# Letting Pool take the weights' low words, and letting the planner run Pool beside VectorE's largest-magnitude steps

## The chip, the cores and the metric

One core of one Trainium2 chip runs the whole kernel: causal attention followed by a feed-forward layer. The metric is device microseconds from the first to the last instruction of a launch. The median of three timed runs of the kernel before is 1076.19 us (1075.35 to 1078.62). The engines are named as in the profile: PE is TensorE, with PEld its weight loads, DVE is VectorE, ACT is ScalarE, POOL is GpSimd (the code calls it Pool), and SP is the engine that issues the transfers.

## The reference

```python
def _attn_ref(q, k, v, s):                      # q, k, v: 8 x 8 x 576 x 64, s: 8 x 8 x 576
    scores = (1.0 / np.sqrt(D)) * np.matmul(q, k.transpose(0, 1, 3, 2))
    cum = np.cumsum(np.maximum(s, 0.0), axis=-1)
    bias = -(cum[:, :, :, None] - cum[:, :, None, :])
    scores = np.where(causal, -1000000000.0, scores + np.minimum(bias, 0.0))
    attn = np.exp(scores - np.max(scores, axis=-1, keepdims=True))
    attn = attn / (np.sum(attn, axis=-1, keepdims=True) + 1e-09)
    return np.matmul(attn, v)

def _moe_ref(x, w_in, w_out):                   # x: 4608 x 512, w_in: 512 x 2048, w_out: 2048 x 512
    h = x @ w_in
    g = np.where(h > 0.0, h, np.exp(np.minimum(h, 0.0)) - 1.0)
    return g @ w_out
```

The attention's output, with its heads side by side, is the `x` of the second function. The two weight matrices arrive as 64-bit floats, everything else as 32-bit floats.

## The kernel before

**Stages.** The attention works on units of one batch, one pair of heads and one head of the pair. Softmax is done in blocks of 128 queries (`softmax_block`): PE makes the scores in a bank `sc` (line 969), DVE adds the mask and takes the row's extreme (line 972, written `CUSTOM_DVE_ANT_0` in the profile and `ISA` in lists of the order, with a second short instruction that reads the accumulator), ACT takes the exponential (line 977), and the block is scaled and cut into two half-precision parts by POOL, DVE or ACT (lines 1016 to 1030). There are 352 such blocks. SP turns the parts by a transfer, and PE multiplies them with the values into a bank `av` (line 1131). The feed-forward layer works on 12 chunks of 384 tokens; a chunk runs over 16 slices `f` of the hidden width. Chunk 0 is done in full precision (`hidden_native`, lines 1301 and 1346). The others are done with each operand cut into two half-precision parts: 12 matmuls of 384 columns for `h` (line 1317), then the activation through ACT and DVE (lines 1281 to 1335: `g`, `h`, `gg`), then 9 matmuls of 512 columns into `o` (line 1354).

**The weights.** 32 pieces of 128 x 512 weights (16 of `w_in`, 16 of `w_out`) are loaded as pairs of 32-bit words by `load_unit`. ACT turns the high word of each into a scaled float (line 638). DVE takes the low word to its top three bits (line 641: multiply by 2 to the -29, clip at 7). DVE joins the two (line 644). Then the piece's largest magnitude is taken by `peak`: on DVE as a `TENSOR_REDUCE` (line 575), or on ACT with an accumulator (line 578). `peak` also serves the values (`vs` and `va`), on DVE alone. When all 32 pieces are there, `weight_scales` makes common scales, and `split_unit` cuts every piece into two half-precision parts `wp` (ACT or POOL for the high part, DVE for the low part at line 659). Only then can chunk 1 and the later ones run.

**What sets the order.** Nothing is ordered by hand. Each step is given to `plan.op` as a list of ways, and a way is an engine, a cost in ns and the code. `Plan.issue` keeps a clock of its own for each engine. For each step it takes the way that would end first, and then it issues the step that could start first (a lower priority number goes first among equals); the order that comes out on each engine is the program's. Two rules of this planner matter here. The planner takes DVE's work with operands in SBUF (named `"DVE-SB"`) and Pool's work to exclude each other: a `port` clock holds the end of the last of either kind, and a step of either kind may start only a little ahead of it (240 ns for `"DVE-SB"`, 120 ns for `"Pool"`). Way `"DVE"` is the same engine without that rule. Costs on DVE count 1.3 times when ways are compared. A change of one cost or way therefore moves the order of all later work on every engine.

Engines work through their instructions in this order, so one that waits holds up all that stand behind it on its engine.

Of the kernel before, what the change touches and what calls it, by code (L numbers as in the profile page):

```python
# [15 lines left out]
ALU = mybir.AluOpType  # L16
# [65 lines left out]
class Plan:  # L82
# [40 lines left out]
    def op(self, prio, ways, reads=(), writes=(), late=()):  # L123

        o = Op()
        o.ways, o.prio, o.filler = ways, (prio, len(self.ops)), False
        o.after, o.before, o.behind, o.bufs, o.new = set(late), [], [], set(), []
        firsts = set()
        for accesses, write in ((reads, False), (writes, True)):
            for a in accesses:  # L130
                b, part = a if isinstance(a, tuple) else (a, None)
                if not b.parts and b not in o.bufs:

                    o.new.append((b, self.place(b)))
                    b.first = o
                firsts.add(b.first)
                if b not in o.bufs:
                    o.bufs.add(b)
                    b.users += 1
                for key, (writers, readers) in b.parts.items():  # L140
                    if part is None or key is None or key == part:
                        o.after.update(writers)
                        if write:
                            o.after.update(readers)
                writers, readers = b.parts.setdefault(part, ([], []))
                if write:
                    if part is None:
                        b.parts = {None: ([o], [])}
                    else:
                        b.parts[part] = ([o], [])  # L150
                else:
                    readers.append(o)
        o.after.discard(o)
        firsts -= o.after | {o}
        for d in o.after:
            d.before.append(o)
        for d in firsts:
            d.behind.append(o)
        o.left, o.ready = len(o.after) + len(firsts), {}
        self.ops.append(o)  # L160
        return o
# [139 lines left out]
def act_s(n):  # L301

    return 205 + n / 1.2
# [26 lines left out]
def kernel(  # L330
# [43 lines left out]
    op = plan.op  # L374
    act, dve, pool, pe_ = nc.scalar, nc.vector, nc.gpsimd, nc.tensor

    def load(prio, dst, src, reads, writes, nbytes, late=(), lag=LAG):
        return op(prio, [("SP", SP_COST, lambda: nc.sync.dma_start(dst(), src()), lag, nbytes)],
                  reads, writes, late)
# [167 lines left out]
    def weight(f, kind):  # L547
        return (w_all[f // W_GROUP], (f, kind)), lambda: w_all[f // W_GROUP].v[:, f % W_GROUP, kind]
# [23 lines left out]
    def peak(prio, n, src, reads, at, axis=mybir.AxisListType.X, aside=None, also=()):  # L572

        col = slice(at, at + 1)
        ways = [("DVE-SB", 100 + 1.04 * n, lambda: dve.tensor_reduce(
            peaks.v[:, col], src(), axis, ALU.max, apply_absolute_value=True))]
        if aside is not None:
            ways.append(("ACT", 480 + n / 1.2, lambda: act.activation(
                aside(), src(), AF.Abs, accum_out=peaks.v[:, col])))
        op(prio, ways, reads, [(peaks, at), *also])  # L580
# [45 lines left out]
    def load_unit(f, kind, src):  # L626

        prio = W0 + WD * f
        a, n = src.shape[1], f"{'io'[kind]}{f}"
        place, value = weight(f, kind)  # L630
        if wide:
            raw = plan.buf(sb, [P, 512, 2], U32, f"w_{n}", tag="io", bufs=N_IO)
            load(prio, lambda: raw.v.rearrange("p (a n) t -> p a (n t)", a=a),
                 lambda: src.bitcast(U32), [], [raw], P * 4096, urgent if f >= N_FREE else ())

            op(prio, [("ACT", act_s(512), lambda: act.activation(
                raw.v[:, :, 1].bitcast(F32), raw.v[:, :, 1].bitcast(F32),
                AF.Prelu, scale=2.0**-112, alpha=2.0**32))], [], [(raw, 1)])  # L640
            op(prio, [("DVE-SB", 430.0, lambda: dve.tensor_scalar(
                raw.v[:, :, 0], raw.v[:, :, 0], 2.0**-29, 7.0, ALU.mult, ALU.min))],
               [], [(raw, 0)])
            op(prio, [("DVE-SB", 700.0, lambda: dve.scalar_tensor_tensor(
                value().bitcast(U32), raw.v[:, :, 1], 3, raw.v[:, :, 0],
                ALU.logical_shift_left, ALU.bitwise_or))], [(raw, 0), (raw, 1)], [place])
        else:
            load(prio, lambda: value().rearrange("p (a n) -> p a n", a=a), lambda: src,
                 [], [place], P * 2048, urgent)
        peak(prio, 512, value, [place], (A_IN, A_OUT)[kind] + f,  # L650
             aside=(lambda: raw.v[:, :, 0].bitcast(F32)) if wide else None, also=[(raw, 0)] if wide else [])
# [11 lines left out]
    def load_weights(f0, f1):  # L663
        wi = w_in.rearrange("(c p) f -> p c f", p=P)
        wo = w_out.rearrange("(f p) (a m) -> f p a m", p=P, a=1)
        for f in range(f0, f1):
            fs = slice(f * P, (f + 1) * P)
            load_unit(f, 0, wi[:, :, fs])
            load_unit(f, 1, wo[f])
# [33 lines left out]
    def prepare_low(u):  # L703

        b, j, prio = u.b, u.j, u.prio
        u.vs = vs[u.turn]
        u.k, clear = (k_first, None) if (b, j) == (0, 0) else low_keys(u.tag)
        u.q = plan.buf(sb, [P, 2 * LOW], F32, f"ql_{u.tag}", tag="qs", bufs=2)
        heads, h0 = slice(2 * j, 2 * j + 2), b * H + 2 * j
        at = slice(HB, HB + 1)  # L710
        load(prio, lambda: u.k.v[:HB], lambda: kT[b, :HB, heads, :LOW], [], [(u.k, "k")], P * LOW * 4)
        load(prio, lambda: u.q.v[:HB], lambda: qT[b, j, :HB, : 2 * LOW], [], [(u.q, "q")], P * LOW * 4)
        op(prio if b or j else -10, [("Pool-M", pool_1(2 * LOW), lambda: pool.memset(u.q.v[HB:], 1.0))],
           [], [(u.q, "ones")])
        if (b, j) > (0, 0):
            op(prio, clear, [], [(u.k, "sums")])

            src = aux if (b, j) == (0, 1) else aux_dram
            o = load(prio, lambda: u.k.v[at],
                     lambda: src.v[h0 : h0 + 2, 0, :LOW],  # L720
                     [(src, 0)], [(u.k, "sums")], 2 * LOW * 4)
        if (b, j) == (0, 1):
            urgent.append(o)
        load(prio, lambda: u.vs.v, lambda: vb[b, j, :, :n_low], [], [u.vs], P * n_low * D * 4)
        peak(prio, n_low * D, lambda: u.vs.v, [u.vs], A_LOW + b * NP + j, mybir.AxisListType.XY)
# [98 lines left out]
    def group_values(u):  # L824

        at = groups.index((u.b, u.blocks[0] > 0))
        prio, first, col = u.prio - V_AHEAD, A_GROUP + at * (NP + 1), 4 + 2 * at
        home = w_parts[NG - 1] if at == 0 else w_all[(at - 1) % 2]
        va = plan.buf(sb, [P, NP, 2 * (NQ + 1), D], F32, f"va_{at}", tag=home.key[1])
        for j in range(NP):  # L830
            load(prio + j, lambda j=j: va.v[:, j], lambda j=j: vb[u.b, j, :, 1:], [], [(va, j)], P * 2 * (NQ + 1) * D * 4)
            peak(prio, 2 * (NQ + 1) * D, lambda j=j: va.v[:, j], [(va, j)], first + j, mybir.AxisListType.XY)
        scales_of(prio, [(first, NP + 1)], col)
        back = scales.v.bitcast(U32)
        op(prio, [("DVE-SB", 100.0, lambda: power(
            back[:, col + 1 : col + 2], back[:, col : col + 1], 2 * 127 - 15))], [(scales, col)], [(scales, col + 1)])
        return va, col
# [600 lines left out]
    while rows:  # L1438
        chunk, left = [], TMAX
        while left:  # L1440
            b, late, r, n = rows.pop(0)
            if n > left:
                rows.insert(0, (b, late, r + left, n - left))
                n = left
# [79 lines left out]
```

## Time and profile before

| what | value |
|---|---|
| timed runs of the kernel before | 1075.35, 1076.19, 1078.62 us |
| span of the profiled execution (the profile names no other time of that execution) | 1076.1 us |
| instructions in the profile | 19708 |
| HBM read and written | 79.66 and 19.32 MB, 92 GB/s over the span |
| transfers in the core's main queue | 155.27 MB, 58.5% of 16 DMA engines' span |
| chain that ended last | PE 70%, DVE 16%, issue 5%, DMA 4%, ACT 2%, POOL 2% |

The busy time of an engine counts the time in which at least one of its instructions runs. Matmuls overlap: one of 384 columns is listed with some 328 ns although the next one starts 162 ns after it. A busy PE can thus still have gaps of up to that length between starts. The chain of waits is followed back from the last instruction, and the waits of an engine name what ended its idle time.

### The profile page before, as it was taken

What the parts mean: (1) busy time and instruction counts of PE and PEld (TensorE: products, weight loads), DVE (VectorE), ACT (ScalarE), POOL (GpSimd) and SP (SyncE); (2) the same over time, 40 slices, a digit from 0 to 9 for tenths busy, and PEclk for the clock granted to TensorE, in tenths of its full rate; (3) what the DMA queues carried; (4) which work ended last, traced back from release to release, by engine and by line L of the source; (5) the groups of instructions that cost most, each with busy time, mean ns of one, the idle gap of its engine ahead of it and who ended that gap; (6) DMA issues with size and microseconds to landing.
All of it is one profiled execution on the core that took longest, in us unless ns stands there. A gap on an engine that the chain in (4) does not pass through costs nothing.

```text
span 1076.1 us, 19708 instructions
## 1 busy us (share of the span) xinstructions
PE 1028.8 (96%) x6014; PEld 597.0 (55%) x6014; DVE 859.3 (80%) x2216; ACT 640.2 (59%) x1511; POOL 443.2 (41%) x687
## 2 busy tenths in 40 slices
PE   8899999899799999999999999999999999999998
PEld 7555555345455555555555555555555655555554
DVE  7787988998788988898898888988898998442433
ACT  5787675547566666655656666665556566444443
POOL 6542443525365645454535545444444544000000
PEclk9999999899899999999999999999999999999999
DMA  6776889526667675675579675867765567210000
GB/s 192 216 223 203 213 213 203 139 65 142 172 149 193 149 171 136 169 179 147 120 168 191 144 162 137 195 159 167 170 168 143 143 156 148 52 60 1 30 1 30
DMA packets 295097, 156.52 MB, mean 145 GB/s; under 512 B 214200, under 2 KB 269776, under 8 KB 294992
## 3 DMA queue, kind: packets, MB, share of 16 engines
q1 hardware_dynamic: 294992, 155.27, 58.5%
q8 instruction: 48, 0.79, 0.3%
q14 instruction: 57, 0.47, 0.2%
HBM read 79.66 MB, written 19.32 MB: 92 GB/s over the span
## 4 chain that ended last, share of the span: by engine, by line
PE 70%; DVE 16%; issue 5%; DMA 4%; ACT 2%; POOL 2%; SPq 1%; DVEq 0%; POOLq 0%; ACTq 0%
PE o L1354 24%; PE h L1317 23%; PE sc L969 8%; PE av L1131 5%; DVE p L1030 4%; PE o L1346 3%; PE h L1301 2%; DVE xl L1270 2%; DVE h L1326 2%; DVE wp L659 1%; DVE gg L1335 1%; DVE p L972 1%; PE trl L791 1%; DMA T<-p 1%; DMA stq<-in_qT_dram 1%
## 5 line engine op out<-in xcount | busy, mean ns | idle before, releaser
L1317 PE MATMUL h<-xh,wp 128*128 128x384 f16 x1408 | 394.1, 329 | 19.4 <-DVE gg L1335 14.0
L1354 PE MATMUL o<-wp,gg 128*128 128x512 f16 x1584 | 390.6, 382 | 0.0
L1317 PEld LDWEIGHTS <-wp 128*128 128x128 f16 x2112 | 198.0, 98 | 177.0 <-issue 35.8
L1317 PE MATMUL h<-xl,wp 128*128 128x384 f16 x704 | 230.8, 328 | 3.9 <-DVE xl L1270 3.9
L1354 PEld LDWEIGHTS <-gg 128*128 128x128 f16 x1584 | 147.2, 99 | 154.0 <-issue 6.8
L1281 ACT ACTIVATE g<-h,cs 128x384 f32<-128x384 f32 x176 | 101.8, 578 | 156.3 <-PE h L1317 145.4
L977 ACT ACTIVATE p<-p,mn 128x192 f32<-128x192 f32 (+1 forms) x232 | 144.2, 622 | 56.6 <-DVE mn L972 49.2
L1326 DVE SCALAR_TENSOR_TENSOR h<-g,cs,h 128x384 f32<-128x384 f32 x176 | 108.5, 617 | 86.8 <-ACT g L1288 85.7
L1030 DVE SCALAR_TENSOR_TENSOR p<-p,sm,p 128x512 f16<-128x512 f32 (+3 forms) x237 | 168.9, 736 | 3.2 <-POOL p L1022 1.1
L1330 ACT ACTIVATE gg<-h 128x384 f16<-128x384 f32 x155 | 75.4, 487 | 93.2 <-DVE h L1326 91.6
L969 PE MATMUL sc<-kh,qs 128*128 128x192 f32 (+2 forms) x272 | 120.0, 444 | 7.7 <-DVE mn L972 7.3
L972 DVE CUSTOM_DVE_ANT_0 p<-sc,maskw 128x192 f32<-128x192 f32 (+1 forms) x232 | 109.6, 480 | 18.8 <-PE sc L969 14.3
L1022 POOL TENSOR_SCALAR p<-p,sm 128x512 f16<-128x512 f32 (+3 forms) x120 | 79.5, 670 | 95.5 <-DVE sm L983 34.0
L1335 DVE SCALAR_TENSOR_TENSOR gg<-h,gg 128x384 f16<-128x384 f32 x176 | 96.9, 550 | 22.0 <-ACT gg L1330 19.3
L969 PE MATMUL sc<-k,q 128*128 128x192 f32 (+2 forms) x272 | 84.4, 313 | 0.5 <-DMA q<-qs 0.5
L411 POOL TENSOR_TENSOR k<-stk,kh 64x576 fp32r<-64x576 f32 x49 | 73.1, 1492 | 24.4 <-ACT kh L392 19.9
L969 PEld LDWEIGHTS sc<-kh,qs 128*128 128x128 f32 x272 | 52.4, 192 | 35.6 <-DVE mn L972 14.5
L1288 ACT ACTIVATE g<-g 128x384 f32<-128x384 f32 x134 | 69.9, 522 | 3.7
L1026 ACT ACTIVATE p<-p,sm 128x512 f16<-128x512 f32 (+3 forms) x100 | 57.4, 594 | 18.5 <-DVE sm L983 8.2
L411 POOL TENSOR_TENSOR qs<-stq,qs 64x512 fp32r<-64x512 f32 (+1 forms) x46 | 52.4, 1139 | 34.0 <-ACT qs L392 23.5
L390 POOL TENSOR_SCALAR qs<-stq 128x256 fp32r<-128x256 f32 (+1 forms) x43 | 24.3, 566 | 88.8 <-PE sc L969 57.5
L1131 PE MATMUL av<-T,v 128*64 128x256 f16 (+5 forms) x896 | 60.2, 286 | 0.0
(179 smaller groups left out, 1414.1 us busy)
## 6 DMA issues: line engine op xcount, KB each, us to landing
stk<-in_kT_dram SPq DMA_DIRECT2D x64, 288.0 KB
va<-in_vb_dram SPq DMA_DIRECT2D x32, 320.0 KB
stq<-in_qT_dram SPq DMA_DIRECT2D x40, 256.0 KB
w_i<-in_w_in_dram SPq DMA_DIRECT2D x16, 512.0 KB
w_o<-in_w_out_dram SPq DMA_DIRECT2D x16, 512.0 KB
out_dram<-ost SPq DMA_DIRECT2D x32, 256.0 KB
x_dram<-x_None SPq DMA_DIRECT2D x20, 288.0 KB
q<-qs SPq DMA_DIRECT2D x40, 128.0 KB
```

Source lines behind the costliest of these rows:

```text
L411: ("Pool", pool_2(n), lambda: pool.tensor_tensor(dst(), src(), hi(), ALU.subtract)),
L969: pe_.matmul(view(sc.v[:, :cw]), l, r, start=n == 0, stop=n == len(pairs) - 1)
L972: op(prio, [("DVE", 84 + dve_p(cw), lambda i=i, sc=sc: dve.tensor_tensor_reduce(pt.v[:, i * cw : (i + 1) * cw], sc.v[:, :cw], mv(i * cw, c ...
L977: op(prio, [("ACT", 480 + w / 1.2, lambda: act.activation(pt.v[:, :w], pt.v[:, :w], AF.Exp, bias=mn.v[:, n - 1 : n], scale=-1.0, accum_out ...
L1022: ("Pool", 160 + 1.04 * n, lambda part=part: pool.tensor_scalar(part(t16, 0), own(part), sm.v[:, r], 1.0, ALU.mult, ALU.mult)),
L1030: ("DVE-SB", dve_2(n), lambda part=part: dve.scalar_tensor_tensor(part(t16, 1), own(part), sm.v[:, r], part(t16, 0), ALU.mult, ALU.subtract)),
L1131: pe_.matmul(av.v[w.h * HB : (w.h + 1) * HB, dst], w.values.v[:, w.h, kb, v], part(w, kb, m), start=kb == 0 and m == 0 and v == 0, stop=kb ...
L1281: op(side, [("ACT", act_c(TC) + (0 if native else 90), lambda: act.activation(g.v[:, :TC], hp.v[:, :TC], AF.Exp, scale=1.0 if native else ...
L1317: pe_.matmul(hp.v[:, :TC], weight_part(f, 0, part)[1]()[:, c * P : (c + 1) * P], xx.v[:, c, :TC], start=(c == 0 and m == 0), stop=(c == NC ...
L1326: op(side, [("DVE", dve_p(TC), lambda: dve.scalar_tensor_tensor(hp.v[:, :TC], g.v[:, :TC], by(2 if sign[0] else 1), hp.v[:, :TC], ALU.mult ...
L1335: op(side, [("DVE", dve_p(TC), lambda: dve.scalar_tensor_tensor(gg.v[:, 1, :TC], hp.v[:, :TC], 2.0**-DOWN, gg.v[:, 0, :TC], ALU.mult, ALU. ...
L1354: pe_.matmul(acc[i].v, gg.v[:, g, tb], weight_part(f, 1, part)[1](), start=(f == 0 and m == 0), stop=(f == NF - 1 and m == 2),)
```

## The change

There are two edits. In `peak` the DVE way is renamed from `"DVE-SB"` to `"DVE"`, with the same cost and the same instruction: the planner no longer keeps Pool's work apart from it. In `load_unit` the step on the low words gets a second way: Pool at 660 ns, with the same arithmetic on the same words.

```diff
@@ def peak
-        ways = [("DVE-SB", 100 + 1.04 * n, lambda: dve.tensor_reduce(
+        ways = [("DVE", 100 + 1.04 * n, lambda: dve.tensor_reduce(
             peaks.v[:, col], src(), axis, ALU.max, apply_absolute_value=True))]
@@ def load_unit
-            op(prio, [("DVE-SB", 430.0, lambda: dve.tensor_scalar(
-                raw.v[:, :, 0], raw.v[:, :, 0], 2.0**-29, 7.0, ALU.mult, ALU.min))],
-               [], [(raw, 0)])
+            op(prio, [
+                ("DVE-SB", 430.0, lambda: dve.tensor_scalar(
+                    raw.v[:, :, 0], raw.v[:, :, 0], 2.0**-29, 7.0, ALU.mult, ALU.min)),
+                ("Pool", 660.0, lambda: pool.tensor_scalar(
+                    raw.v[:, :, 0], raw.v[:, :, 0], 2.0**-29, 7.0, ALU.mult, ALU.min)),
+            ], [], [(raw, 0)])
```

All lines behind the second edit stand three lower than before (line 972 becomes 975); the low words' step is line 642 on DVE and line 644 on Pool.

The planner gives 22 of the 32 low words' steps to Pool and leaves 10 on DVE. The largest magnitudes of the weights, of which DVE had 16 and ACT 16, now stand 22 on DVE and 10 on ACT. The other ways change in small numbers: over the whole program DVE has 2218 instructions before and 2224 now, ACT 1209 and 1190, POOL 692 and 707, and PE 10334 and 10336 (two more of the matmuls that only fill time at the start).

The first place is on POOL, at the second weight piece (`w_o_289` is its buffer; `pl` and `p` are softmax blocks, `v` a part of the values). Before:

```order
L990 TENSOR_SCALAR pl_1_295<-pl_1_295,sml_1_303 128x128
L990 TENSOR_SCALAR p_174<-p_174,sml_1_303 128x320
L402 TENSOR_SCALAR v_0_0_0_397<-va_134,scales 128x5x64
L402 TENSOR_SCALAR v_1_0_0_407<-va_134,scales 128x5x64 x2
L538 MEMSET p_87 128x64
```

Now:

```order
L993 TENSOR_SCALAR pl_1_295<-pl_1_295,sml_1_303 128x128
L993 TENSOR_SCALAR p_174<-p_174,sml_1_303 128x320
L644 TENSOR_SCALAR w_o_289<-w_o_289 128x512
L402 TENSOR_SCALAR v_0_0_0_402<-va_134,scales 128x5x64
L402 TENSOR_SCALAR v_1_0_0_414<-va_134,scales 128x5x64 x2
L538 MEMSET p_87 128x64
```

The low words' step stands between the scaling of softmax blocks, which waits for DVE's reciprocals, and the values.

The second place is on DVE, where the weights are cut after the common scales are known (`wp` are the parts, `wa` the pieces; `h`, `g` and `gg` belong to chunk 1; line 972 is a softmax block). Before, from the tenth of the 32 cuts on:

```order
L1326 SCALAR_TENSOR_TENSOR h_2_2380<-g_2_2411,cs_2238,h_2_2380 128x384
L659 SCALAR_TENSOR_TENSOR wp_2271<-wa_1049,scales,wp_2271 128x512 x2
L1335 SCALAR_TENSOR_TENSOR gg_2_2444<-h_2_2380,gg_2_2444 128x384
L1326 SCALAR_TENSOR_TENSOR h_3_2423<-g_3_2446,cs_2238,h_3_2423 128x384
L659 SCALAR_TENSOR_TENSOR wp_2271<-wa_1049,scales,wp_2271 128x512 x2
L1335 SCALAR_TENSOR_TENSOR gg_3_2461<-h_3_2423,gg_3_2461 128x384
L972 ISA p_174,mn_2_1_0_3_2472<-sc_2_1_0_3_0_2245,maskw 128x288
L972 ISA mn_2_1_0_3_2472 128x1
L659 SCALAR_TENSOR_TENSOR wp_2271<-wa_1049,scales,wp_2271 128x512 x2
L659 SCALAR_TENSOR_TENSOR wp_2302<-wa_1428,scales,wp_2302 128x512 x2
```

Now, from the third cut on:

```order
L662 SCALAR_TENSOR_TENSOR wp_2171<-wa_430,scales,wp_2171 128x512 x4
L1295 TENSOR_SCALAR g_0_2306<-g_0_2306 128x384
L662 SCALAR_TENSOR_TENSOR wp_2208<-wa_1006,scales,wp_2208 128x512
L1329 SCALAR_TENSOR_TENSOR h_0_2275<-g_0_2306,cs_2183,h_0_2275 128x384
L662 SCALAR_TENSOR_TENSOR wp_2208<-wa_1006,scales,wp_2208 128x512 x2
L1338 SCALAR_TENSOR_TENSOR gg_0_2332<-h_0_2275,gg_0_2332 128x384
L1329 SCALAR_TENSOR_TENSOR h_1_2302<-g_1_2336,cs_2183,h_1_2302 128x384
L662 SCALAR_TENSOR_TENSOR wp_2208<-wa_1006,scales,wp_2208 128x512 x2
L1338 SCALAR_TENSOR_TENSOR gg_1_2356<-h_1_2302,gg_1_2356 128x384
L662 SCALAR_TENSOR_TENSOR wp_2208<-wa_1006,scales,wp_2208 128x512 x3
```

Before, the 32 cuts stand between the 89th and the 94th softmax block; now all 32 stand behind the 88th with no block between them.

The third place is on PE, at the attention's last products. The number at the end of `h` is the slice `f` of the tenth chunk (chunk 9). Before:

```order
L1131 MATMUL av_3_1_2_11846<-T_3_1_2_11793,v_3_0_2_11532 64x64
L1354 LDWEIGHTS gg_11_11822
L1354 MATMUL o_2_11178<-wp_2302,gg_11_11822 128x512
L1354 LDWEIGHTS gg_11_11822
L1354 MATMUL o_2_11178<-wp_2302,gg_11_11822 128x512
L1354 LDWEIGHTS gg_11_11822
L1354 MATMUL o_2_11178<-wp_2302,gg_11_11822 128x512
L1317 LDWEIGHTS wp_2343
L1317 MATMUL h_13_11884<-xh,wp_2343 128x384
```

Now:

```order
L1134 MATMUL av_3_1_2_11923<-T_3_1_2_11869,v_3_0_2_11611 64x64
L1320 LDWEIGHTS wp_2256
L1320 MATMUL h_15_11899<-xh,wp_2256 128x384
L1320 LDWEIGHTS wp_2256
L1320 MATMUL h_15_11899<-xl,wp_2256 128x384
L1320 LDWEIGHTS wp_2256
```

Behind the last product of the attention stood 420 matmuls into `h` and 327 into `o`; now 390 and 306 stand there. The chunk is some two and a half slices further on when the attention ends.

## The prediction, made before the changed kernel ran

> **What bounds the kernel now.** I read the page's first part, then the busy times by stage, then the waits of PE, then the end of the chain.
>
> ```profile
> span 1076.1 us, 19708 instructions
> ...
> PE 1028.8 (96%) x6014; PEld 597.0 (55%) x6014; DVE 859.3 (80%) x2216; ACT 640.2 (59%) x1511; POOL 443.2 (41%) x687
> ```
>
> ```profile
> core 0: us, PE busy (x) PEld busy (x) DVE busy (x) ACT busy (x) POOL busy (x), PEclk, DMA share, GB/s
> 0.00:90.00 90.00, 80.40 (x496) 55.26 (x497) 73.19 (x252) 63.46 (x203) 47.33 (x122) 1.00 0.71 211
> 90.00:180.00 90.00, 89.54 (x357) 49.85 (x356) 76.51 (x195) 58.97 (x147) 32.39 (x51) 1.00 0.80 209
> 180.00:240.00 60.00, 52.75 (x244) 26.60 (x243) 55.69 (x113) 32.37 (x65) 27.71 (x33) 0.94 0.46 115
> 240.00:720.00 480.00, 456.34 (x2779) 267.23 (x2778) 417.91 (x1115) 298.13 (x721) 237.66 (x341) 0.99 0.68 160
> 720.00:930.00 210.00, 207.96 (x1365) 123.27 (x1364) 183.91 (x453) 125.08 (x262) 93.82 (x135) 1.00 0.64 152
> 930.00:1076.00 146.00, 141.84 (x782) 74.77 (x779) 52.11 (x92) 62.21 (x116) 4.26 (x6) 1.00 0.07 23
> ```
>
> PE is full from 90 to 180 us (89.54 of 90) and again from 720 us on (207.96 of 210; after 930 almost nothing but feed-forward matmuls is left). It has room in the other three stages: 9.6 us up to 90, 7.2 from 180 to 240, 23.7 from 240 to 720, and gaps shorter than a matmul's listed length come on top (its record outlasts the start of the next). In those stages DVE is the next fullest, with 81%, 93% and 87%, while POOL is at 53% and 36% in the two stages that read weights.
>
> ```profile
> PE h L1317 <- DVE gg L1335: 14.0, 18, 3.1
> PE sc L969 <- DVE mn L972: 7.8, 10, 2.5
> PE h L1317 <- DVE xl L1270: 3.9, 6, 1.5
> ```
>
> These are PE's three longest waits (us in total, times, longest), all for DVE. So I read the kernel as PE's sum of matmuls plus gaps that DVE's order sets. A change can gain only what closes such gaps; PE's own work stays, since its list has the same matmuls.
>
> **What the change takes off DVE.** The step itself:
>
> ```profile
> L641 DVE TENSOR_SCALAR w_i<-w_i x16: 398/428/651, 19.7 to 167.3; 128x512 uint32<-128x512 uint32 x16
> L641 DVE TENSOR_SCALAR w_o<-w_o x16: 409/434/1640, 28.5 to 175.2; 128x512 uint32<-128x512 uint32 x16
> ```
>
> ```profile
> L575 DVE TENSOR_REDUCE peaks<-wa 128x1 f32<-128x512 f32 x16 | 10.8, 677 | 0.2
> ...
> L641 DVE TENSOR_SCALAR w_o<-w_o 128x512 uint32<-128x512 uint32 x16 | 9.4, 589 | 2.0 <-DMA w_o<-in_w_out_dram 2.0
> ...
> L641 DVE TENSOR_SCALAR w_i<-w_i 128x512 uint32<-128x512 uint32 x16 | 7.2, 450 | 1.1 <-DMA w_i<-in_w_in_dram 1.1
> ```
>
> The 32 steps cost 9.4 + 7.2 = 16.6 us, 0.519 each, against medians of 0.428 and 0.434: a few are stretched. 22 go to Pool, 22 x 0.519 = 11.4 us. The ten that stay I take at the median, 0.9 us less in all. Together 12.3 us leave DVE. Six more largest magnitudes come to it from ACT, 6 x 0.677 = 4.1 us. The planner fills the rest of the room: summing each engine's list at the means of the groups by line and shape, other work that moves to DVE up to the last softmax block is 19.8 us, and 8.5 us move away. The largest of it:
>
> ```profile
> L1024 DVE TENSOR_SCALAR p<-p,sm 128x512 f16<-128x512 f32 (+3 forms) x52 | 26.2, 506 | 1.5 <-DVE sm L983 0.3
> ...
> L1292 DVE TENSOR_SCALAR g<-g 128x384 f32<-128x384 f32 x58 | 26.1, 451 | 10.7 <-ACT g L1281 10.6
> ...
> L410 DVE TENSOR_TENSOR k<-stk,kh 64x576 fp32r<-64x576 f32 x15 | 11.6, 773 | 1.1 <-POOL kh L390 0.7 <-ACT kh L392 0.3
> ...
> L418 DVE COPY tl<-trl 128x128 f32<-128x128 f32 (+2 forms) x21 | 7.9, 377 | 6.3 <-PE trl L791 4.6 <-PE trl L775 1.4
> ...
> L1145 DVE TENSOR_SCALAR x_None<-av,scales 128x512 f32<-128x512 f32 x9 | 6.7, 747 | 5.0 <-PE av L1131 4.8
> ```
>
> Twelve more copies out of the banks (4.9 us by their shapes), six more rests of q and k (4.7), six more scalings of softmax blocks (3.2), four more outputs of the attention (2.5); nine fewer steps on `g` (4.1). Net on DVE up to the last block: -12.3 + 4.1 + 19.8 - 8.5 = +3.1 us. Up to the 100th block, where the weights have just been cut, the same sum is -12.3 + 4.1 - 0.6 = -8.8 (the -0.6 is the other work), and up to the 280th it wavers between -5 and 0, of which I take -1.5. So DVE is relieved early, and the planner gives it back later, with ACT and POOL as partners.
>
> **What this does to the end.** Two estimates, since the bound changes at 720 us.
>
> ```profile
> 0.00:180.00 180.00, 34.95 (x176) 1.00 0.76 210
> 180.00:720.00 540.00, 89.32 (x384) 0.98 0.66 155
> ```
>
> ```profile
> L972 DVE CUSTOM_DVE_ANT_0 p<-sc,maskw,mn x64: 500/513/519, 114.7 to 919.7; 128x288 f32<-128x288 f32 x64
> ```
>
> ```profile
> L1131 PE MATMUL av<-T,v x896: 192/273/404, 142.4 to 932.6; 128*64 128x256 f16 x44, 128*64 128x192 f16 x38, 128*64 128x64 f16 x26, 128*64 128x512 f16 x24
> ```
>
> ```profile
> 960.86 1.95 PE h L1317 x12
> 962.81 1.94 PE o L1354 x9
> ```
>
> The first fence is the softmax line alone by stages: (176 + 384) / 2 instructions a block make 280 blocks before 720 us; the last starts at 919.7, and the attention's last product at 932.6. The fourth gives PE's pace: 1.95 / 12 = 0.1625 us for a matmul into `h`, 1.94 / 9 = 0.2156 into `o`.
>
> - If DVE's list sets when the attention ends, the end of attention comes 3.1 us later. Behind the last product stand 30 fewer matmuls into `h` and 21 fewer into `o`: 30 x 0.1625 + 21 x 0.2156 = 4.9 + 4.5 = 9.4 us less. Sum 3.1 - 9.4 = -6.3.
> - If PE is the bound from the 280th block on, what counts is the state there: DVE 1.5 us ahead, and feed-forward matmuls worth 1.1 us more already issued (counted in PE's lists at the pace above). Sum -1.5 - 1.1 = -2.6.
>
> I take the middle, -4.4: against the execution's own span, 1076.1 - 4.4 = **1071.7 us**. The span is 0.1 us below the median of the timed runs (1076.19), so the same figure stands for the median. About 0.3%, 3.2 us, is what a measurement of this kernel can tell from no change; the forecast lies just beyond it.
>
> **The Pool step's price.** No uint32 work on POOL is in the trace, nor a step of two words. The nearest rows:
>
> ```profile
> L390 POOL TENSOR_SCALAR qs<-stq 128x512 fp32r<-128x512 f32 x21 | 14.2, 675 | 46.9 <-DMA stq<-in_qT_dram 19.2 <-PE sc L969 17.6 <-issue 6.3
> ...
> L411 POOL TENSOR_TENSOR qs<-stq,qs 64x512 fp32r<-64x512 f32 x28 | 37.2, 1329 | 32.5 <-ACT qs L392 23.5 <-DVE sm L982 4.7 <-PE sc L969 1.5
> ...
> L402 POOL TENSOR_SCALAR wp<-wa,scales 128x512 f16<-128x512 f32 x17 | 15.5, 932 | 2.4 <-DVE scales L614 2.4
> ```
>
> I take 0.675, the row of the same operation and size; 1.329, the two-operand row, is the far end, and 0.45, what DVE needs, the near one. At 0.675 the 22 steps are 14.9 us in 180 us in which POOL works 79.7, beside other work. The joining of the words (line 644 before) now waits for Pool. DVE keeps its order, so behind a waiting join stand softmax steps (line 972), for which ACT's exponentials and PE's next scores wait. Per step, 1.329 - 0.675 = 0.65 us would be exposed at most, 22 x 0.65 = 14.4 us; at 0.45 nothing more is won, since the planner counts 0.66 anyway.
>
> [...]
>
> **The renamed way.** It costs and wins nothing by itself if Pool's work really runs beside it:
>
> ```profile
> 44.47 1.47 POOL L990 TENSOR_SCALAR pl<-pl,sml 128x320 f32<-128x320 f32 x1
> ...
> 45.87 0.67 DVE L575 TENSOR_REDUCE peaks<-wa 128x1 f32<-128x512 f32 x1
> ```
>
> The reduction began within Pool's step and took 0.67 us, its mean (677 ns). So the planner's new freedom is real, and its worth is inside the lists above.
>
> **The rivals.**
>
> *No change (1076).* The relief ends at the 100th block; from 90 to 180 us PE is full, and from 720 us on again. If the gaps between (7.2 + 23.7 us) depend on chains rather than on DVE's sum, the early 8.8 us become slack and the tail's 9.4 us come back as a later end of attention. For it speaks that DVE's whole list is not shorter (2224 against 2218 instructions); against it that PE's longest waits are for DVE. It gives 1076.1 - 0.
>
> *Slower (1082).* Pool's steps hold up DVE.
>
> ```profile
> 133.88 1.40 POOL L411 TENSOR_TENSOR k<-stk,kh 64x576 fp32r<-64x576 f32 x1 [1.55 <-ACT kh L392]
> 133.92 1.64 DVE L641 TENSOR_SCALAR w_o<-w_o 128x512 uint32<-128x512 uint32 x1
> ```
>
> Here Pool began 0.04 us earlier, and a step of 0.43 us on DVE took 1.64. With 22 more Pool steps of 0.932 (the slow row above), met by DVE on average half-way, 22 x 0.47 = 10.3 us come to DVE: 1071.7 + 10.3 = 1082.0. It needs a loss of (4.4 + 3.2) / 22 = 0.35 us a step to be slower by more than 3.2. For it: the row above, and joins that wait for a Pool queue which itself waits for DVE. Against it: the present stretching is 0.519 - 0.43 = 0.09 us a step, and the medians show most steps untouched. [...]
>
> That the change does not do what it says is excluded: 22 of 32 steps stand on Pool in the list.
>
> **How the numbers follow.** Forecast 50%, no change 28%, slower 22%; these are also the chances of faster by over 0.3%, within it, and slower by over it. The low end is 1064: 12.3 us off DVE with nothing put back, 1076.1 - 12.3 = 1063.8. The high end is 1084, between the slower rival (1082.0) and the far price of the Pool step (1071.7 + 14.4 = 1086.1), which I leave out with the little that lies below the low end. So the range is 1064 to 1084.
>
> **What would show it.** Right: 22 Pool steps near 0.68 us, joins without waits for POOL, the 100th softmax block some 5 to 9 us earlier, PE's idle time before 90 us and from 180 to 240 us smaller, and the last product of the attention at most 3 us later than 932.6 with a tail 9 us shorter. Wrong: joins waiting for POOL in the waits, longer two-input steps on DVE between 20 and 180 us, or the lead at the 100th block gone by the 280th. Only the lists' sums carry the forecast's sign; a wait of 2 us in a later stage that this trace cannot show would turn it into no change.

## The result and the profile after

The change made the kernel slower: 1091.66 us (median of 4 runs, 1090.25 to 1092.64) against 1075.77 us for the kernel before (4 runs), a ratio of 1.0146, 95% interval 1.0128 to 1.0165. The forecast was 1071.7 us, with a range up to 1084.

The page of the kernel after, span and first part (busy time, share of the span, instructions):

```profile
span 1090.3 us, 19717 instructions
...
PE 1032.9 (95%) x6016; PEld 601.2 (55%) x6016; DVE 861.1 (79%) x2222; ACT 631.3 (58%) x1486; POOL 487.3 (45%) x702
```

Two readings. The span grew by 14.2 us, the median by 15.9: where a run lists both its time and its span, the time is 1.8 us more (1092.12 for the 1090.3 here), so the profiled execution before was some 2 us slower than the median. The growth of the span can be split: PE's idle time went from 1076.1 - 1028.8 = 47.3 us to 1090.3 - 1032.9 = 57.4 (+10.1), and PE's busy time rose by 4.1 us for the same matmuls, with a granted clock of 0.986 over the span against 0.990. And POOL, at 443.2 us before, has 44 us more, where the forecast put 14.9 there for the step.

The same stretches as before the change, kernel after (us, busy time and count of each engine, granted clock, DMA):

```profile
0.00:90.00 90.00, 77.05 (x472) 52.87 (x472) 67.43 (x229) 57.89 (x184) 65.94 (x130) 0.98 0.69 201
90.00:180.00 90.00, 86.37 (x345) 46.97 (x341) 71.29 (x181) 53.18 (x135) 59.85 (x63) 1.00 0.80 211
180.00:240.00 60.00, 55.61 (x245) 29.50 (x246) 55.93 (x118) 33.77 (x68) 25.52 (x34) 0.94 0.35 106
240.00:720.00 480.00, 455.20 (x2777) 269.37 (x2776) 416.61 (x1119) 294.17 (x711) 233.11 (x329) 0.98 0.66 157
720.00:930.00 210.00, 202.69 (x1306) 118.86 (x1305) 184.37 (x451) 121.49 (x259) 94.40 (x135) 0.99 0.64 155
```

In the two stages that read weights POOL rose from 47.33 and 32.39 to 65.94 and 59.85 us. DVE is less busy there (73.19 to 67.43, 76.51 to 71.29), but not only relieved: it also has 37 fewer instructions in these 180 us (410 against 447), where the edits account for some 16 (22 steps away, six largest magnitudes more). The rest is work that comes later. PE lost 3.4 and 3.2 us there, and from 720 to 930 another 5.3.

The line of the step on Pool (its own queue's row, then duration min/median/max in ns, first and last start), with what waited for it:

```profile
L644 POOL TENSOR_SCALAR w_i<-w_i x12: 1972/2010/2457, 35.4 to 161.1; 128x512 uint32<-128x512 uint32 x12
L644 POOL TENSOR_SCALAR w_o<-w_o x10: 1987/2014/2307, 23.6 to 167.7; 128x512 uint32<-128x512 uint32 x10
...
  DVE wa L647: 14.6, 13
```

All 22 steps ran on Pool, as listed, but each took 2.01 us, three times the 0.675 that I took and half as much again as the far end, 1.329. The joins on DVE (line 647 now) waited 13 times for them, 14.6 us in total. In one of these waits DVE stood idle for 1.87 us before the join began at 170.09 us; its next two steps began at 170.69 and 171.16 us.

PE's longest waits, kernel after:

```profile
PE h L1320 <- DVE gg L1338: 17.8, 15, 3.5
PE sc L972 <- DVE mn L975: 7.0, 11, 1.3
PE h L1320 <- ACT xh L403: 3.5, 1, 3.5
PE trl L778 <- POOL pl L993: 3.5, 5, 1.0
PE sc_None L972 <- DMA q2s<-qs_None: 2.6, 1, 2.6
```

The first rose from 14.0 us. The fourth is Pool's own list: softmax scalings (line 993) that come late. Only one of the five stands directly behind a low-word step, but with a cheap step in the same order (x_cheap below) this wait is 0.2 us in place of 3.5. The third and the fifth are single waits that end at 300.2 and 296.2 us; the experiments come back to them. The third was there before the change, too:

```profile
PE h L1317 <- ACT xh L403: 3.4, 1, 3.4
```

The reductions that the planner may now set beside Pool's work, and the end of the attention:

```profile
L575 DVE TENSOR_REDUCE peaks<-wa x22: 645/676/687, 28.4 to 181.6; 128x1 f32<-128x512 f32 x22
```

```profile
L1134 PE MATMUL av<-T,v x896: 192/273/636, 148.3 to 956.3; 128*64 128x256 f16 x44, 128*64 128x192 f16 x37, 128*64 128x64 f16 x27, 128*64 128x448 f16 x25
```

No reduction over `wa` took more than 687 ns, although by the times of the trace 19 of the 22 ran beside an instruction on POOL (8 of 16 before), so the renamed way does what it says. The attention's last product starts at 956.3 us against 932.6, 23.7 later; behind it stand 1090.3 - 956.3 = 134.0 us against 143.5, a tail 9.5 us shorter (forecast: 9.4).

### The profile page after: what moved, and what is told of

The parts are those of the page before. It is cut to its first block, busy times and chain, and to the rows that moved or that the text cites. A ratio compares the mean times of both kernels' runs of the same rounds, so it can differ in the third digit from the quotient of the medians.

```text
span 1090.3 us, 19717 instructions
## 1 busy us (share of the span) xinstructions
PE 1032.9 (95%) x6016; PEld 601.2 (55%) x6016; DVE 861.1 (79%) x2222; ACT 631.3 (58%) x1486; POOL 487.3 (45%) x702
## 4 chain that ended last, share of the span: by engine, by line
PE 53%; DVE 12%; DMA 3%; issue 3%; ACT 2%; SPq 1%; POOL 0%; DVEq 0%; POOLq 0%; ACTq 0%
PE o L1357 22%; PE h L1320 21%; PE sc L972 5%; PE av L1134 4%; DVE p L1033 3%; DVE p L975 1%; DVE h L1329 1%; DVE gg L1338 1%; DVE v L858 1%; DVE xl L1273 1%; DMA T<-p 1%; DMA x_dram<-x_None 1%; DMA stq_None<-in_qT_dram 1%; ACT g L1284 0%; SPq L378 0%
## 5 line engine op out<-in xcount | busy, mean ns | idle before, releaser
L1025 POOL TENSOR_SCALAR p<-p,sm 128x64 f16<-128x64 f32 (+3 forms) x121 | 79.3, 661 | 129.7 <-DVE sm L986 59.0
L1333 ACT ACTIVATE gg<-h 128x384 f16<-128x384 f32 x159 | 77.7, 488 | 91.5 <-DVE h L1329 90.0
L1291 ACT ACTIVATE g<-g 128x384 f32<-128x384 f32 x141 | 73.6, 522 | 3.8
L411 POOL TENSOR_TENSOR k<-stk,kh 64x576 fp32r<-64x576 f32 x46 | 68.4, 1488 | 14.1 <-ACT kh L392 12.6
L1134 PE MATMUL av<-T,v 128*64 128x256 f16 (+5 forms) x896 | 63.8, 291 | 3.2 <-DMA T<-p 2.3
L1029 ACT ACTIVATE p<-p,sm 128x512 f16<-128x512 f32 (+3 forms) x92 | 53.0, 597 | 18.9 <-issue 8.1
L1134 PEld LDWEIGHTS <-v 128*64 128x64 f16 x896 | 47.1, 111 | 28.1 <-issue 13.4
L402 POOL TENSOR_SCALAR xh<-xc,cs 128x384 f16<-128x384 f32 x30 | 19.8, 668 | 94.2 <-PE h L1320 93.7
```

What stands on the lines that cost most here:

```text
L1025: ("Pool", 160 + 1.04 * n, lambda part=part: pool.tensor_scalar(part(t16, 0), own(part), sm.v[:, r], 1.0, ALU.mult, ALU.mult)),
L1134: pe_.matmul(av.v[w.h * HB : (w.h + 1) * HB, dst], w.values.v[:, w.h, kb, v], part(w, kb, m), start=kb == 0 and m == 0 and v == 0, stop=kb ...
L1333: ("ACT", act_c(TC), lambda: act.activation(gg.v[:, 0, :TC], hp.v[:, :TC], AF.Copy, scale=2.0**-DOWN)),
```

## The experiments

All ratios are to runs of the kernel before on the same chip at the same time.

| run | what it is | us | ratio, 95% interval |
|---|---|---|---|
| (after) | the change | 1091.66 | 1.0146 [1.0128, 1.0165] |
| e_peak_alone | renamed way alone | 1068.42 | 0.9944 [0.9926, 0.9962] |
| e_low_alone | step on Pool alone | 1066.80 | 0.9932 [0.9913, 0.9951] |
| x_cheap | change, Pool step 0.66 us | 1080.42 | 1.0044 [1.0030, 1.0058] |
| x_mid | change, Pool step 1.33 us | 1087.18 | 1.0104 [1.0086, 1.0122] |
| x_dve | change's order, steps issued on DVE | 1082.42 | 1.0065 [1.0049, 1.0082] |
| e_low_cheap | step on Pool alone, 0.67 us | 1060.17 | 0.9856 [0.9843, 0.9869] |
| x_670_cheap | both edits, cheap step, planner's 670 | 1069.45 | 0.9943 [0.9920, 0.9965] |
| x_670 | both edits, planner's 670 | 1078.40 | 1.0026 [1.0008, 1.0045] |
| b_435 | kernel before, planner's 430 as 435 | 1075.58 | 1.0010 [0.9995, 1.0026] |
| b_428 | kernel before, planner's 430 as 428 | 1069.17 | 0.9951 [0.9936, 0.9967] |

m1_forms (1101.8 us) and m2_forms (1091.4) are the kernel before with more instructions and only measure these; their totals say nothing. The 1076 us expected for m1_forms did not come, as its instructions ran at the start of Pool's list and not at its end.

### Why the step costs 2.0 us: m1_forms

```diff
+    for _ in range(2):
+        pool.tensor_scalar(d2, s2, 2.0**-29, 7.0, ALU.mult, ALU.min)
...
+        pool.tensor_scalar(d1.bitcast(F32), s1.bitcast(F32), 2.0**-29, 7.0, ALU.mult, ALU.min)
+        pool.tensor_scalar(d1.bitcast(F32), s1.bitcast(F32), 2.0**-29, 7.0, ALU.mult, ALU.mult)
...
+        pool.tensor_scalar(d2, s2, 2.0**-29, 7.0, ALU.mult, ALU.mult)
```

> The kernel before, plus 18 Pool instructions on a scratch tile behind Pool's last one, where the trace of before has Pool idle; nine forms of a 128x512 step with two constants, twice each, which differ from the step on the low words in one thing: type (uint32, float32, uint16 in), step between elements (one word or two), last operation (min or mult). The changed kernel's step took 2010 ns at the median where I had priced 675. Theory 1, the integer type: both uint32 forms, of one word and of two, take about 2.0 us, and both float32 forms with min about 0.65 us; a form with uint32 on one side alone lies between. Theory 2, the step of two words: both forms of two words take about 2.0 us and both of one word about 0.65. Theory 3, the minimum: all forms with min take about 2.0 us, those with mult 0.65. Time of the whole: 1076 us within 2, since PE's last matmuls end after them.

The instructions on the scratch tile, m1_forms: the step as it is; the same in f32 and without the stride; then two multiplications in f32, and two on every second uint32 word.

```profile
L1469 POOL TENSOR_SCALAR m_src<-m_src x2: 2006/2006/2006, 6.2 to 29.4; 128x512 uint32<-128x512 uint32 x2
...
L1472 POOL TENSOR_SCALAR m_src<-m_src x2: 1919/1920/1920, 19.3 to 35.6; 128x512 f32<-128x512 f32 x2
L1473 POOL TENSOR_SCALAR m_src<-m_src x2: 619/620/622, 21.3 to 37.6; 128x512 f32<-128x512 f32 x2
...
L1477 POOL TENSOR_SCALAR m_src<-m_src x2: 641/646/651, 28.7 to 46.1; 128x512 uint32<-128x512 uint32 x2
```

Neither the integers nor the stride of 8 bytes cost anything worth naming (646 against 620 ns). With `min` as second operation the same instruction took three times as long (1920 against 620 ns in f32), whatever the type: the five forms that are not shown, all with `min`, have medians of 1.96 to 2.05 us. So the third theory holds: 0.65 us with two multiplications, 2.01 with the limit.

### Which operations are dear: m2_forms

```diff
+    for _ in range(2):
+        pool.tensor_scalar(g1, f1, 2.0**-29, None, ALU.mult)
+        pool.tensor_scalar(g1, f1, 7.0, None, ALU.min)
+        pool.tensor_scalar(g1, f1, 7.0, 2.0**-29, ALU.min, ALU.mult)
+        pool.tensor_scalar(g1, f1, 2.0**-29, 0.0, ALU.mult, ALU.max)
+        pool.tensor_scalar(g1, f1, 2.0**-29, 1.0, ALU.mult, ALU.add)
+        pool.tensor_scalar(g1, f1, 2.0**-29, 7.0, ALU.mult, ALU.min)
```

> The changed kernel with twelve more Pool instructions on a scratch tile (note that the total says nothing then): 128x512 in f32, twice each of one multiplication; one limit (min); limit and multiplication; multiplication and max; multiplication and addition; and multiplication and limit as in the step. If it is the comparison that costs (min and max alike, in either place): 1.9 to 2.0 us for the four with one, 0.6 us for the two without. If only a limit in second place costs: 1.9 to 2.0 for the last alone (and for max if that counts as one), 0.6 for the others.

The text says "changed kernel"; the instructions were added to the kernel before. The six forms, in the order of the diff:

```profile
L1467 POOL TENSOR_SCALAR m_src<-m_src x2: 1493/1496/1498, 6.3 to 23.0; 128x512 f32<-128x512 f32 x2
L1468 POOL TENSOR_SCALAR m_src<-m_src x2: 1492/1532/1572, 13.3 to 25.1; 128x512 f32<-128x512 f32 x2
L1469 POOL TENSOR_SCALAR m_src<-m_src x2: 1926/1964/2003, 14.9 to 26.7; 128x512 f32<-128x512 f32 x2
L1470 POOL TENSOR_SCALAR m_src<-m_src x2: 1930/1934/1938, 18.3 to 28.7; 128x512 f32<-128x512 f32 x2
L1471 POOL TENSOR_SCALAR m_src<-m_src x2: 620/620/620, 20.3 to 30.7; 128x512 f32<-128x512 f32 x2
L1472 POOL TENSOR_SCALAR m_src<-m_src x2: 1924/1924/1925, 21.0 to 31.4; 128x512 f32<-128x512 f32 x2
```

Both readings fell in part. A comparison cost time in every pair that had one: `min` in either place, and `max` as second operation, where alone it was tried (1.92 to 1.96 us); but a single multiplication was dear too (1.50 us), and so was a single limit (1.53). Quick were, of the forms tried, only the pairs of arithmetic: multiplication with multiplication or with addition (0.62). The row that I took as price, line 390 with 675 ns, is such a pair: the kernel multiplies by a second factor of 1.0 on Pool, where its way on DVE has no second operation. The trace names both `TENSOR_SCALAR`; only the code shows the difference.

### Each edit alone: e_peak_alone, e_low_alone

```diff
-        ways = [("DVE-SB", 100 + 1.04 * n, lambda: dve.tensor_reduce(
+        ways = [("DVE", 100 + 1.04 * n, lambda: dve.tensor_reduce(
```

> The first edit alone: the planner lets Pool work while DVE takes the largest magnitudes; the low words stay on DVE. If the Pool step's price is the whole loss, this is within 0.5% of the kernel before, 1071 to 1081 us. If the loosened rule is itself the loss (Pool's work beside a reduction that it holds up, or a worse order), it is slower by most of the 15.9 us, 1085 us or more. My theory: 1076.

```diff
+                ("Pool", 660.0, lambda: pool.tensor_scalar(
+                    raw.v[:, :, 0], raw.v[:, :, 0], 2.0**-29, 7.0, ALU.mult, ALU.min)),
```

> The second edit alone: the low words may go to Pool at the planner's 660 ns, the largest magnitudes keep the old rule. 14 of 32 steps go to Pool here, not 22. If the Pool step's price is the loss, it is in proportion to the steps, 14/22 of 15.9 us: about +10 us, 1086 us (1081 to 1089). If the loss is the loosened rule, it is 1076 within 4.

Each alone made the kernel faster, by 0.6 and 0.7%. With 1068.42 us the first lies below both of its cases, whose lower one began at 1071. The second did so with 14 steps on Pool at a median of 2.02 us each, for which joins waited 8.0 us. So a dear step alone cannot be the whole loss: what I expected from price in proportion to the steps missed. The order in which the planner lays the work became the second suspect.

### Price and order apart: x_cheap, x_mid, x_dve, e_low_cheap

The change's lists, instruction for instruction, with another Pool way (x_cheap); in e_low_cheap the same line stands in the order of e_low_alone:

```diff
-                    raw.v[:, :, 0], raw.v[:, :, 0], 2.0**-29, 7.0, ALU.mult, ALU.min)),
+                    raw.v[:, :, 0], raw.v[:, :, 0], 2.0**-29, 0.9375, ALU.mult, ALU.mult)),
```

> The changed kernel, instruction for instruction in the same order, with one thing altered: the Pool way of the low-word step multiplies by 2^-29 and then by 0.9375 in place of the limit at 7 (the largest word still gives 7; the three bits of some values come out one lower), and in m1_forms a step of that form took 0.64 us in place of 2.0. The planner goes on counting 660 ns. Theory A (the price is the loss): the order is as good as it was forecast, and 22 x (2.0 - 0.65) = 30 us of Pool's time in the first 170 us made it late: 1066 to 1075 us, joins waiting under 4 us for POOL, the 100th softmax block 5 us or more before that of the kernel before. Theory B (the order is the loss: the two edits together let the planner move too much, whatever a step takes): 1083 us or more.

The step and the joins' wait, x_cheap:

```profile
L644 POOL TENSOR_SCALAR w_i<-w_i x12: 642/666/838, 33.6 to 151.3; 128x512 uint32<-128x512 uint32 x12
L644 POOL TENSOR_SCALAR w_o<-w_o x10: 647/663/852, 22.9 to 156.1; 128x512 uint32<-128x512 uint32 x10
...
  DVE wa L647: 1.4, 2
```

Its first two stages, and the one from 720 us on:

```profile
0.00:90.00 90.00, 81.77 (x511) 55.22 (x512) 73.72 (x249) 62.94 (x202) 56.26 (x138) 1.00 0.73 216
90.00:180.00 90.00, 87.76 (x343) 49.49 (x342) 74.04 (x196) 55.69 (x136) 45.41 (x64) 1.00 0.80 209
...
720.00:930.00 210.00, 205.16 (x1349) 121.26 (x1348) 184.69 (x447) 121.67 (x258) 91.40 (x131) 1.00 0.62 147
```

The result lies between the two theories, and so both have a share. The joins wait 1.4 us, as the first theory had it, but the 100th softmax block is only 2.6 us early, not 5. Against the change 22 x (2.01 - 0.665) = 29.6 us left Pool and 1091.66 - 1080.42 = 11.2 us the total, 0.38 for one. 6.1 us of it is PE's idle time before 180 us (77.05 to 81.77 and 86.37 to 87.76), where the joins no longer wait. But with the step at just the price that I had taken, the kernel is still 0.44% slower than before, where I had forecast 0.4% faster.

x_mid puts two quick instructions at each place (medians 0.66 and 0.67 us):

```diff
+                ("Pool", 660.0, lambda: (pool.tensor_scalar(
+                    raw.v[:, :, 0], raw.v[:, :, 0], 2.0**-29, 0.9375, ALU.mult, ALU.mult),
+                    pool.tensor_scalar(
+                    raw.v[:, :, 0], raw.v[:, :, 0], 1.0, 1.0, ALU.mult, ALU.mult))[1]),
```

> The changed kernel's order again, with the cheap step issued twice at each of the 22 places (the second multiplies by 1 and 1), so that a Pool step costs some 1.28 us, near the far end of the range the prediction gave (1.329). Theory A with a loss in proportion: half-way between x_cheap and the changed kernel, about 1081 us. Theory A with slack (Pool's queue takes it in until it is full): within 4 us of x_cheap. Theory B: 1083 us or more.

1087.18 us, 6.8 more than x_cheap for 22 x 0.67 = 14.7 us of Pool: 0.46 for one. From there to the change it is 4.5 us for 15, 0.30 for one. The price reaches the end roughly in proportion; there is no slack that takes in the first part of it. The 1081 us of the proportional theory would need an x_cheap near 1071; half-way between the two as measured is 1086.0. The order theory's "1083 or more" holds in number, but x_cheap has the same order and 6.8 us less, so the step's price does count.

> Edit 2 alone (e_low_alone, same order, 14 steps on Pool) with the same cheap form of the Pool step. Theory A1 (each microsecond of a Pool step reaches the end wherever it stands, as the 20 us over 22 x 1.35 us in the changed kernel would have it, 0.67 us for one): 14 x 1.35 x 0.67 = 12.7 us less than e_low_alone, 1054 us. Theory A2 (that order has slack at its Pool steps, and a step's price counts only where the Pool queue is full): within 4 us of e_low_alone, 1063 to 1068 us.

1060.17 us, 6.6 below e_low_alone for 14 x 1.35 = 18.9 us of Pool: 0.35 for one (0.43 by the two ratios, since the two ran at different times). That is about the same rate as in the change, not the 0.67 nor the near nothing of the two theories. This is the fastest version of the study, 1.44% below the kernel before.

x_dve issues the 22 steps on DVE at the same places:

```diff
-                ("Pool", 660.0, lambda: pool.tensor_scalar(
+                ("Pool", 660.0, lambda: dve.tensor_scalar(
```

> The changed kernel's order, but the 22 steps are issued on DVE at the same places of the program (0.43 us each with the limit at 7, as before the change), while the planner believes them on Pool. 22 x 0.43 = 9.5 us come back to DVE's list, none to Pool's. Theory A (the price on Pool is the loss): faster than the changed kernel by over 8 us, between 1068 and 1082 us. Theory B (the order is the loss): 1088 us or more.

1082.42 us, 0.4 above the upper end of the first theory and far from the second's 1088. With none of these steps on Pool this order is still 0.65% slower than the kernel before. What is left is the order itself, together with 9.5 us of steps on DVE at places where the planner had put none; this run does not part the two. x_cheap, without these steps on DVE, is 0.44% slower.

### Where the order might lose: x_670_cheap, x_670, b_435, b_428

The timeline of the kernel after at that place (start, duration, engine, line, work, idle time before it and what ended it):

```profile
282.66 0.33 PE L1320 MATMUL h<-xh,wp 128*128 128x384 f16 x1
...
290.82 0.54 SPq L378 DMA_DIRECT2D x_dram<-x_None  x1
...
291.21 0.47 PE L972 MATMUL sc<-kh,qs 128*128 128x448 f32 x1 [1.32 <-DVE mn L975]
...
295.99 0.45 SPq L378 DMA_DIRECT2D xc<-x_dram  x1
...
299.53 0.60 ACT L403 ACTIVATE xh<-xc,cs 128x384 f16<-128x384 f32 x1
...
300.18 0.48 PE L1320 MATMUL h<-xh,wp 128*128 128x384 f16 x1 [3.51 <-ACT xh L403]
```

From 282.99 to 300.18 us no feed-forward matmul runs: the rows whose attention is done are used up, and the next ones must first be stored (290.82), read back (295.99) and cut (299.53). PE has only scores and products, which wait on short chains. At 300.18 us a matmul of 384 columns is listed with 0.48 us in place of 0.33. That does not come of the gap of 3.51 us just before it, since the granted clock (the third number from the end) had fallen to one half some 8 us earlier and is 0.50 from 294 to 304 us:

```profile
288.00:292.00 4.00, 2.22 (x18) 1.57 (x12) 4.00 (x10) 1.63 (x5) 3.26 (x8) 1.00 0.40 94
292.00:294.00 2.00, 1.11 (x5) 0.74 (x3) 1.34 (x6) 1.08 (x4) 1.57 (x3) 0.59 0.96 254
294.00:296.00 2.00, 0.00 (x0) 0.00 (x0) 1.77 (x9) 1.15 (x3) 0.21 (x1) 0.50 0.72 164
```

In the 4 us before the fall PE was busy for 2.22 us, and its longest gap was the 1.32 us at 291.21. What stands ahead of the fall is thus a stretch in which PE was a little over half busy; what made the clock fall is not shown. The granted clock of the longer stretches below is a mean.

The stretch from 260 to 310 us, first the kernel before, then after:

```profile
260.00:310.00 50.00, 43.11 (x251) 24.72 (x250) 41.10 (x112) 30.25 (x71) 21.48 (x33) 0.90 0.63 157
```

```profile
260.00:310.00 50.00, 36.50 (x222) 22.08 (x219) 40.21 (x106) 27.33 (x66) 20.41 (x31) 0.83 0.67 162
```

The kernel before already has a hole here (6.9 us idle, clock 0.90); the change doubles it (13.5 us, 0.83). x_cheap has it alike (13.4 us, 0.83), while with one edit alone it is 4.2 (e_peak_alone) and 2.8 us (e_low_alone), at 1.00. In PE's lists one can count how much feed-forward work is laid ahead of it. So I altered the planner's numbers by a few ns. No instruction's work changes by that, but the planner lays out the program anew: in another order, and with some steps on other engines (by the pages POOL has 702 instructions in x_cheap and 679 in x_670_cheap). What is called order below is both.

```diff
-                ("Pool", 660.0, lambda: pool.tensor_scalar(
+                ("Pool", 670.0, lambda: pool.tensor_scalar(
```

> Both edits with the cheap Pool form of x_cheap, and one number of the planner altered: the Pool way counts 670 ns in place of 660. 21 steps go to Pool in place of 22. What differs is the order: in PE's list 409 feed-forward matmuls stand ahead of the 160th score matmul, against 466 in the changed kernel and x_cheap (and none between the 160th and the 170th there), 463 before, 421 and 415 with one edit. Theory S (the stock of feed-forward work: a list that has spent its ready rows by then leaves PE dry between 260 and 310 us, as the traces show: idle 6.9 us at a granted clock of 0.90 before, 13.4 at 0.83 in x_cheap, 4.2 and 2.8 at 1.00 with one edit): under 5 us idle there at 1.00, total 1060 to 1068 us. Theory E (the two edits do not go together, whatever the order): 1076 to 1084 us.

```profile
260.00:310.00 50.00, 44.35 (x282) 26.79 (x281) 44.13 (x119) 29.43 (x72) 23.86 (x37) 1.00 0.64 158
```

The hole is gone but for 5.6 us, the clock stays at 1.00, and the total is 1069.45 us, 11.0 below x_cheap: both edits do go together. It is 1.5 us above what the stock theory allowed (and the idle time a little over its 5 us), 6.5 below what the other did. Most of the gain is PE's pace and not its idle time. By the pages the spans are 1077.5 us in x_cheap and 1068.4 here: PE's idle time fell by 2.4 us (48.8 to 46.4), its busy time by 6.7 (1028.7 to 1022.0) with as many instructions, and the granted clock over the span rose from 0.987 to 0.995.

> Both edits as in the changed kernel, with the limit at 7 and its step of 2.0 us on Pool, and only the planner's number 670 in place of 660 (21 steps on Pool, the order of x_670_cheap). Price: 21 x 1.36 us at 0.35 to 0.50 of a microsecond each, 10 to 14 us more than x_670_cheap. Theory S: 1070 to 1082 us, 10 us or more below the changed kernel. Theory E: 1086 to 1094 us.

1078.40 us, 13.3 below the change with the same two edits, the same form of the step and one step fewer on Pool; 9.0 above x_670_cheap for 21 x 1.34 = 28.1 us of Pool, 0.32 for one, a little under the 10 to 14 expected.

And the kernel before with neither edit:

```diff
-            op(prio, [("DVE-SB", 430.0, lambda: dve.tensor_scalar(
+            op(prio, [("DVE-SB", 435.0, lambda: dve.tensor_scalar(
```

> The kernel before, with neither edit; only the planner's number for the low-word step on DVE is 435 ns in place of 430. No instruction changes its kind, and none goes to Pool; the order is planned anew, and 466 feed-forward matmuls stand ahead of the 160th score matmul and 466 ahead of the 170th, as in the changed kernel (463 and 472 before). Theory S: PE idle 12 us or more between 260 and 310 us at a granted clock under 0.87, total 1080 to 1088 us. Theory E (the edits make the order bad): within 3 us of the kernel before.

```profile
260.00:310.00 50.00, 36.41 (x208) 21.91 (x207) 38.97 (x112) 31.14 (x72) 22.34 (x31) 0.83 0.67 161
```

The hole came as the list had it, 13.6 us at 0.83, without any edit. The total did not follow: 1075.58 us, the same as before within 0.3%, not 1080 to 1088. So a hole there does not settle the total. It is a loss only as far as it isn't given back, and here it was: PE's idle time in this stretch is 6.7 us longer than before, over the whole span only 2.0 (1076.7 - 1027.4 = 49.3 against 47.3). The attention's last product starts later, but b_435 has 126.2 us behind that start where the kernel before has 143.5 and the change 134.0. In the change, too, PE is busy for only 1.1 us less from 240 to 720 us, hole included (455.20 against 456.34), so how much of its loss comes from the hole is not shown. Nor did all steps keep their engine, as I had written (POOL 687 instructions before, 669 here).

> The same with 428 ns in place of 430: 448 feed-forward matmuls ahead of the 160th score matmul, 472 ahead of the 170th. Theory S: PE idle 2 to 5 us between 260 and 310 us, total 1064 to 1071 us. Theory E: within 3 us of the kernel before.

```profile
260.00:310.00 50.00, 45.58 (x271) 26.11 (x269) 38.78 (x104) 30.29 (x72) 22.25 (x32) 0.93 0.61 152
```

4.4 us idle in that stretch at 0.93, and 1069.17 us, as expected. So a number altered by 2 ns is worth as much as the first edit alone (0.9951 against 0.9944).

What stays open: which feature of an order makes it quick or slow (the stock theory told the total right in x_670 and b_428, nearly in x_670_cheap, and wrong in b_435, where the stretches outside made up for the hole), and whether the price of the step reaches PE more through the waiting joins or through Pool's own scalings behind it.

## Why the prediction was wrong, point by point

- **What bounds the kernel**: right in its outline (PE's sum plus gaps), too coarse in its stages. I read 240 to 720 us as one stretch with 23.7 us of room, "in those stages DVE is the next fullest", and priced that room by DVE's list. 6.9 us of it lay in 50 us around 285, where the longest wait, 3.4 of them, was for the next rows (`xh`) and not for a step of DVE, and where the granted clock fell as well (0.90).
- **22 steps leave DVE**: right. The ten that stay have medians of 426 and 430 ns.
- **The Pool step's price: this is the step that failed most.** "I take 0.675, the row of the same operation and size; 1.329, the two-operand row, is the far end." It was 2.01. The row was of the same operation by the trace's name only; its pair of operations was another. With it joins waited for Pool, which was one of my signs of being wrong. In the change's own order the difference is worth 11.2 us, of 20.0 by which the forecast missed. The extra time was 1.34 us a step where I allowed 0.65 at most, but only 0.3 to 0.5 of it reached the end where I let all of it do so. The two errors offset each other by luck: my far bound of 14.4 us does hold the 11.2.
- **The lists' sums**: the second failed step; either of the two alone would have left the time in the range (1071.7 + 11.2 = 1082.9, and 1080.42 in x_cheap). With the step at the price taken (x_cheap) the total is 8.7 us above the forecast. The instruction of the softmax line that I counted as block 100 starts 2.6 us earlier than before, not 8.8, and block 352 10.4 us later, not 3.1. The lead was there at first: block 80 starts 9.2 us earlier (145.6 against 154.7 us), block 88 only 1.2. From block 100 to block 352 it loses 13.0 us, 11.9 were forecast, so what failed is the lead at block 100. My other estimate took PE as the bound from block 280 on, with a lead of 1.5 us there; the lead was 0.3 (717.3 against 717.6), and from 720 to 930 us PE is idle for 4.8 us in x_cheap where it was for 2.0 before. Adding up an engine's list says nothing of where its work stands. With nothing changed but the laying-out (and one step of 22), x_670_cheap is 11.0 us below x_cheap; b_428 is 5.2 below the kernel before, b_435 the same as it.
- **The tail**: right, 9.5 us shorter for 9.4.
- **The renamed way**: right; the reductions took 676 ns beside Pool as 677 before. Alone the edit is worth 0.6% all the same (e_peak_alone), by the new order that it brings.
- **The slower rival** had the sign. Of its two mechanisms the joins that wait for Pool were shown (14.6 us after, 1.4 in x_cheap). The other, DVE held up by Pool's steps, shows no more than before: the low-word steps on DVE keep medians of 426 and 430 ns, and the joins have means of 716 and 712 ns as against 713 and 718, though a few are stretched in both (the longest 1029 ns, before 1230). Its threshold, 0.35 us lost per step, was passed: 11.2 / 22 = 0.51 by the price alone.

## What to carry to other kernels

A row prices a new instruction only if its operations match, not just its name (here 0.675 us by the row and 2.01 run): read the code behind the row, and where a planner counts on the number, measure it first (told 2010 ns, this planner puts no step on Pool, and its lists are those of e_peak_alone). Where a planner lays out the whole program anew, one order before and one after do not show what an edit is worth: nudge a cost by a few ns in both and see how far the total moves (here by 1 to 13 us). Look in PE's idle time for a short stretch where it lacks rows, and not only for the engine that is fullest on average, and look at PE's busy time as well: for the same matmuls it was 1022.0 us at a granted clock of 0.995 and 1032.9 at 0.986.

## What the runs showed of the hardware

On Pool, a 128x512 step with two scalars took 0.62 us for multiplication with multiplication or addition, 1.92 to 2.05 us with a min in either place or a max in the second, 1.50 us for one multiplication alone and 1.53 for one min alone (m1_forms, m2_forms). So the pair of multiplications ran 2.4 times as quick as a single one (620 against 1496 ns). Packed f32 and every second word of uint32 were less than 5% apart in the quick form (620 and 646 ns).

The granted clock of TensorE fell to one half at some 292 us of the changed kernel, after 4 us in which PE was busy for 2.22 us and had no gap over 1.32 us.
